# Row maxima of two heads as products, and another order of weight blocks, in an attention and feed-forward kernel

## The chip, the cores and the metric

The kernel runs on one core of a Trainium2 chip. The metric is device microseconds of one execution. Work is done by TensorE (PE, products into PSUM), VectorE (DVE), ScalarE (ACT), GpSimd (POOL) and the DMA engines, whose transfers are here issued by SyncE (SP) alone, one after the other in one queue.

## The reference

Three stages follow one another: attention with a decay, a mixing and feed-forward step, and a second attention by four experts, of which two are chosen for each row. The change touches the first and the part of the second that runs beside it.

```python
# stage 1: q, k, v [4, 8, 576, 64], f [4, 8, 576]
scores = scale * np.matmul(q, k.transpose(0, 1, 3, 2))
cum = np.cumsum(np.log(np.clip(f, 0.0001, 1.0)), axis=-1)
scores = np.where(causal, -1e9, scores + cum[:, :, :, None] - cum[:, :, None, :])
scores = scores - np.max(scores, axis=-1, keepdims=True)
attn = np.exp(scores)
attn = attn / (np.sum(attn, axis=-1, keepdims=True) + 1e-09)
x = np.matmul(attn, v)            # then [4, 576, 512]
# stage 2: U [576, 32], V [32, 576], w_ch1 [512, 2048], w_ch2 [2048, 512]
h = x.transpose(0, 2, 1) @ U @ V
u = x + h.transpose(0, 2, 1)
x = u + np.maximum(u @ w_ch1, 0.0) @ w_ch2
# stage 3: gate, top 2 of 4 experts, causal attention of each, weighted sum
```

## The kernel before

Stage 1 has 32 heads, in 16 pairs; a pair's two heads lie in one set of tiles. Each head has a planned slot of SLOT = 8.4 us. All work of the slots is written as events: `put(h, us, do)` places `do` at `us` in head h's slot, `early(us, do)` places it ahead of the first slot, which begins at FIRST = 15.6. The events are sorted by their planned time (line 1401), and that order is the order in which each engine (PE, DVE, ACT, SP, POOL) executes its instructions. The planned times are only a table that sorts; nothing waits for a clock.

A head goes through these steps:

- **Load and split.** `load_qk` (L865) loads q and k of a pair, 576 KB, into `aside` or `room`. `split_high` (L883 to L887) casts them on ACT into a high part, `split_moves` (L895 to L918) moves rows to other partitions by transfers of 144 KB within the on-chip memory and puts the sums of the decay (4.5 KB, L901) beside them, `split_low` (L932, POOL) makes the low parts. So each head has four tiles: qa, qb, ka, kb.
- **Row maxima.** `last_rows` (L201) and `first_rows_of` (L219) make rough scores, `last_max` (L206) and four `first_max` (L227) take their maxima on DVE into mx, `turn_max` (L233) turns mx on PE into a 5x128 tile mt, `put_row` (L239) copies it on ACT to mr and a transfer of 2.5 KB (L243) puts it as the last row into qa, so that the score products subtract it.
- **Scores.** `score_products` (L285) has a part u = 0 with two pieces of 288 columns and a part u = 1 with four pieces; for each piece there are two products, qa with ka and qb with kb. Exponentials on ACT (L305) and a split into a high cast (L310, ACT) and a low rest (L313, DVE) follow. The odd heads of the first five pairs (NPLAIN) are kept without that split.
- **Values.** Largest absolute value (`value_max`, L363), a turn on PE (`value_turn`, amt, L368), a power of two (`value_power`, L375 to L377), a spread on PE (`value_spread`, rsp, L383), then factors and splits of the values. Weighted sums L341 to L345, or L357.

Between these steps lies work for later stages. `mix_weights` prepares U and V: `low_bits` (L442, L443 on ACT) and `join_bits` (L449, L450 on DVE) put 32-bit words together from two halves, for U (ur, u), for V's two parts (vraw, vst). `weight_events` does the same for eight blocks of the feed-forward weights, t = 0 to 7, from slot 3 on: a read of 512 KB into raw (L457), low bits, join into wst, a cast (L1318, ACT), and a subtraction (L1320, DVE). `busy` (L1358) issues filler products of 128 columns that nobody reads. From slot 10 on the feed-forward runs between the heads (L704, L710, L720); behind head 31, at some 266 us, it runs alone, then stage 3.

## Time and profile before

| | us |
|---|---|
| median of 3 runs | 786.77 (786.45 to 787.19) |
| the profiled execution's own time | 787.25 |
| its span (first to last instruction) | 785.5 |
| first score product of head 0, 1, 2 | 16.77, 23.35, 31.14 |
| first score product of head 6, 14, 31 | 60.62, 126.53, 266.04 |
| first maxima (L206) of head 3, 6, 14 | 30.29, 50.93, 115.69 |

A slot of a head is read from its first product at L285 of 288 columns to that of the next head. The maxima of head n are made two heads ahead, so L206 of head 6 lies in slot 4. A timeline row reads: start, duration, engine, line, operation, output<-input, shapes, count, and in brackets how long the engine was idle before it and what ended that.

### The profile page before, as it was taken

How to read it: one execution, taken by the hardware profiler on the slowest of the kernel's cores; microseconds unless marked ns; L12 is line 12 of the kernel's file. 1: busy time of each engine (PE TensorE's matmuls, PEld its weight loads, DVE VectorE, ACT ScalarE, POOL GpSimd, SP SyncE). 2: the span in 40 equal slices, each digit the busy share in tenths (PEclk: the TensorE clock that was granted, in tenths of full speed). 3: DMA queues.
4: the chain of work that ended last, by engine and by line, in shares of the span. 5: the costliest groups of instructions: out<-in, count | busy, mean ns of one | idle time of the engine just before them, and what ended most of it. 6: DMA issues, size and time to landing. Idle time of an engine off the chain costs nothing.

```text
span 785.5 us, 19296 instructions
## 1 busy us (share of the span) xinstructions
PE 752.3 (96%) x7399; PEld 649.0 (83%) x7399; DVE 598.5 (76%) x1659; ACT 436.1 (56%) x893; POOL 201.9 (26%) x357
## 2 busy tenths in 40 slices
PE   4899999999999999999999999999999999999996
PEld 4799888989998999877777777777778888878873
DVE  6889999999999959988773685366644688887763
ACT  6778887877786725644421242113312366776673
POOL 8734466665564200000020000000000611111110
PEclk9999999999999999999999999999999999999999
DMA  5668665566563165844133224300103475344322
GB/s 163 174 195 227 194 179 169 178 183 180 172 188 116 61 197 184 266 145 168 54 99 109 73 80 158 113 1 1 62 31 76 120 182 139 76 118 97 91 75 95
DMA packets 65708, 101.97 MB, mean 130 GB/s; under 512 B 8864, under 2 KB 43664, under 8 KB 65616
## 3 DMA queue, kind: packets, MB, share of 16 engines
q1 hardware_dynamic: 65248, 100.09, 43.0%
q8 instruction: 58, 0.95, 0.5%
q10 hardware_dynamic: 368, 0.66, 0.3%
q14 instruction: 34, 0.28, 0.1%
HBM read 53.25 MB, written 23.74 MB: 98 GB/s over the span
## 4 chain that ended last, share of the span: by engine, by line
PE 53%; DVE 2%; ACT 1%; issue 0%; DMA 0%; ACTq 0%; DVEq 0%
PE cps L720 17%; PE hps L704 16%; PE pq L1636 6%; PE pv L1680 3%; PE sc L285 3%; PE po L1732 2%; PE ub L219 1%; PE av L341 1%; PE av L345 1%; PE av L343 1%; PE pos L1732 1%; PE ua L201 0%; DVE ph L313 0%; ACT pf L305 0%; DMA out_dram<-ost 0%
## 5 line engine op out<-in xcount | busy, mean ns | idle before, releaser
L709 ACT ACTIVATE hh<-hps 128x288 f16<-128x288 f32 (+1 forms) x128 | 52.4, 410 | 210.6 <-PE hps L704 186.1
L710 DVE SCALAR_TENSOR_TENSOR hl<-hps,hh 128x288 f16<-128x288 f32 (+1 forms) x128 | 58.2, 454 | 79.5 <-ACT hh L709 79.1
L227 DVE CUSTOM_DVE_ANT_0 ub<-ub,maskm 128x448 f32<-128x448 f32 x192 | 82.4, 429 | 2.3 <-PE ub L219 0.7
L285 PE MATMUL sc<-qa,ka 128*128 128x288 f32 (+4 forms) x288 | 72.0, 309 | 1.6 <-DMA qa<-mr 1.1
L726 DVE SCALAR_TENSOR_TENSOR yc<-cps,back,yc 128x288 f32<-128x288 f32 x96 | 49.3, 514 | 24.5 <-PE cps L720 23.0
L285 PE MATMUL sc<-qb,kb 128*128 128x288 f32 (+4 forms) x288 | 63.5, 302 | 0.0
L341 PEld LDWEIGHTS <-ph 128*128 128x128 f16 x645 | 58.9, 97 | 1.2 <-DVE o L422 0.6
L345 PEld LDWEIGHTS <-ph 128*128 128x128 f16 x645 | 59.3, 97 | 0.4 <-DVE ph L313 0.4
L343 PEld LDWEIGHTS <-ph 128*128 128x128 f16 x645 | 59.3, 98 | 0.3
L1863 POOL TENSOR_SCALAR_AFFINE_SELECT pf<-pf 128x128 f32<-128x128 f32 (+1 forms) x80 | 23.9, 318 | 116.3 <-ACT pf L305 115.6
L285 PEld LDWEIGHTS sc<-qb,kb 128*128 128x128 f32 x288 | 52.3, 189 | 1.5
L206 DVE CUSTOM_DVE_ANT_0 ua<-ua,maskm 128x576 f32<-128x576 f32 x48 | 36.5, 761 | 21.0 <-PE ua L201 12.3
L313 DVE TENSOR_TENSOR ph<-pf,ph 128x512 f16<-128x512 f32 (+1 forms) x66 | 47.6, 734 | 6.4 <-ACT ph L310 6.4
L285 PEld LDWEIGHTS sc<-qa,ka 128*128 128x128 f32 x288 | 48.8, 189 | 3.7 <-issue 1.2
L313 DVE TENSOR_TENSOR ph<-aside,ph 128x512 f16<-128x512 f32 (+1 forms) x63 | 49.8, 802 | 1.2 <-ACT ph L310 1.0
L1056 POOL TENSOR_SCALAR_AFFINE_SELECT aside<-aside 128x128 f32<-128x128 f32 (+1 forms) x80 | 39.6, 514 | 38.5 <-ACT aside L305 29.9
L305 ACT ACTIVATE aside<-sc 128x512 f32<-128x512 f32 (+1 forms) x63 | 38.7, 617 | 18.3 <-PE sc L285 16.5
L720 PE MATMUL cps<-hh,w16b 128*128 128x288 f16 x256 | 48.3, 286 | 0.3 <-DVE hl L710 0.3
L720 PE MATMUL cps<-hh,w1lf 128*128 128x288 f16 x256 | 48.4, 286 | 0.0
L720 PE MATMUL cps<-hh,w16a 128*128 128x288 f16 x256 | 48.4, 286 | 0.0
L305 ACT ACTIVATE pf<-sc 128x512 f32<-128x512 f32 (+1 forms) x66 | 39.7, 609 | 13.1 <-PE sc L285 9.4
L720 PEld LDWEIGHTS <-w16b 128*128 128x128 f16 x384 | 37.4, 98 | 10.2 <-issue 0.8
(281 smaller groups left out, 2464.4 us busy)
## 6 DMA issues: line engine op xcount, KB each, us to landing
raw<-in_w_dram SPq DMA_DIRECT2D x32, 512.0 KB
ust<-udram SPq DMA_DIRECT2D x13, 576.0 KB
ydram<-yc SPq DMA_DIRECT2D x10, 576.0 KB
aside<-in_qk_dram SPq DMA_DIRECT2D x8, 576.0 KB
room<-in_qk_dram SPq DMA_DIRECT2D x8, 576.0 KB
udram<-ustage SPq DMA_DIRECT2D x16, 288.0 KB
ydram<-ust SPq DMA_DIRECT2D x8, 576.0 KB
yc<-ydram SPq DMA_DIRECT2D x8, 576.0 KB
```

What stands on the lines that cost most here:

```text
L227: nc.vector.tensor_tensor_reduce(ub[:, bk, off:off + w], ub[:, bk, off:off + w], maskm[:, S - w:S], 1.0, NEG, OP.add, OP.max, mx[:, t:t + 1])
L285: nc.tensor.matmul(ps[:, bk, off:off + w], wa, xa, start=bk not in banks[:n], stop=bk not in banks[n + 1:])
L305: nc.scalar.activation(pf[:, 0:S].rearrange("p (c n) -> p c n", c=2) if whole else pf[:, 0:n], view, AF.Exp, scale=ISC)
L313: nc.vector.tensor_tensor(pl[:, o0:o0 + n], pf[:, 0:n], ph[:, o0:o0 + n], OP.subtract)
L341: nc.tensor.matmul(av[:, it, :], ph[:, c:c + P], vh[:, jt, :], start=first, stop=False)
L343: nc.tensor.matmul(av[:, it, 0:64], ph[:, c:c + P], vl[:, jt, :], start=False, stop=False)
L345: nc.tensor.matmul(av[:, it, :], pl[:, c:c + P], vh[:, jt, :], start=False, stop=last)
L704: nc.tensor.matmul(ph[:], wa[:, k, fs], xa[:, k], start=n == 0, stop=n == 3 * KT - 1)
L709: after(lambda: nc.scalar.activation(hh[:], ph[:], AF.Relu), lambda: nc.vector.scalar_tensor_tensor(hl[:], ph[:], 0.0, high, OP.max, OP.su ...
L710: lambda: nc.vector.scalar_tensor_tensor(hl[:], ph[:], 0.0, high, OP.max, OP.subtract))
L720: nc.tensor.matmul(pc[:], wa[:, t, dsl], xa[:], start=n == 0, stop=n == 3 * FT - 1)
L726: nc.vector.scalar_tensor_tensor(yc[:, d, :], pc[:], back, yc[:, d, :], OP.mult, OP.add)
```

## The change

It has five parts.

1. **Maxima of heads 0 and 1.** No copy and no transfer: `spread_rows` writes, on VectorE, a 5x640 tile with row t of mt at the columns of tile t and zeros elsewhere (mt minus a constant, times the unit matrix), and `score_products` adds for each piece a product of five rows, a tile of -1 with that tile. The four `first_max` of a head stand directly behind one another.
2. **The front.** FIRST is 13.6. Fillers: 76 + 6 + 12 + 8 ahead of slot 0, 8 + 6 in slot 0, 8 + 14 in slots 1 and 2 as before, none in slots 3 to 9. The table of the exponentials is loaded early. Pair 0's amt, power and spread stand ahead of the maxima of head 0. On SP's queue the load of pair 1 stands behind two moves that stood behind it.
3. **Values of other pairs.** The turn (amt) goes from 4.54 to 4.7 and the power from 5.6 to 6.42 of the slot.
4. **U and V.** Bits and joins go to later slots; so do their spread, casts and lows. The split of pair 2's first head goes from slot 0 to slot 1.
5. **Weight blocks.** Every block one slot earlier; for those of an odd slot the read goes to 6.5, the bits to the next slot's 3.2, the join to its 6.45, the cast to the slot behind at 1.4.

The core of the diff:

```diff
-FIRST = 15.6
+FIRST = 13.6
...
+    def spread_rows(mt, w):
+
+        rows = w[0:NT].rearrange("o k n -> o (k n)")[:, 0:SP_]
+        nc.vector.scalar_tensor_tensor(
+            rows.rearrange("o (t p) -> o t p", p=P), mt[:].unsqueeze(1).to_broadcast([NT, NT, P]),
+            PSCALE_LN / ISC, ident[0:NT, 0:NT].unsqueeze(2).to_broadcast([NT, NT, P]),
+            OP.subtract, OP.mult)
+        return rows
+
...
-    def score_products(hb, u, select=False):
+    def score_products(hb, u, select=False, rows=None):
...
+        if rows is not None:
+            todo += [(W[0][1][0:NT, 0, 0:P], rows[:, SP_ - S + i0:SP_ - S + i0 + w], bk, off, w)
+                     for jt, i0, bk, w, off in pieces]
...
         nc.sync.dma_start(f32(qa[lo_, :]), f32(qb[hi_, :]))
         nc.sync.dma_start(f32(ka[lo_, :S]), f32(khigh[hi_, :]))
         if p == 0:
-            rows()
+            split_moves(0, 2)
             load_qk(1)
-            split_moves(0, 2)
         nc.sync.dma_start(f32(kb[lo_, :S]), f32(khigh[hi_, :]))
...
-            st[u] = score_products(hb, u, select)
+            st[u] = score_products(hb, u, select, first_rows.get(h))
...
                 early(us, rows, n)
             early((9.2, 12.45)[h], lambda: last_max(st[0], st["mx"]))
             for n, t in enumerate((3, 2, 1, 0)):
-                early((9.8, 13.1)[h] + 0.6 * n, first, t)
+                early((9.8, 13.1)[h] + 0.02 * n, first, t)
...
         if h == 0:
             early(12.2, turn)
-            early(12.6, lambda: put_row(hb, st["mt"], True))
+            early(12.95, lambda: first_rows.update({h: spread_rows(st["mt"], W[0][2 * h])}))
         else:
             put(h - 1, 0.55, turn)
-            put(h - 1, 1.3, lambda: put_row(hb, st["mt"], True))
+            if h == 1:
+                put(0, 0.58, lambda: first_rows.update({h: spread_rows(st["mt"], W[0][2 * h])}))
+            else:
+                put(h - 1, 1.3, lambda: put_row(hb, st["mt"], True))
...
             early(6.6, step, "am", None, lambda _: value_max(vr))
-            put(0, 0.3, step, "amt", "am", value_turn)
-            put(0, 0.35, step, "full", "amt", value_power)
-            put(0, 2.05, step, "rp", "full", value_spread)
+            early(8.4, step, "amt", "am", value_turn)
+            early(8.45, step, "full", "amt", value_power)
+            early(8.75, step, "rp", "full", value_spread)
...
-        put(h, 4.54, step, "amt", "am", value_turn)
-        put(h, 5.6, step, "full", "amt", value_power)
+        put(h, 4.7, step, "amt", "am", value_turn)
+        put(h, 6.42, step, "full", "amt", value_power)
         put(h + 1, 0.57, step, "rp", "full", value_spread)
         put(h + 1, 2.2, factor)
...
             h = 2 * (p - 2) + j
-            put(h, 4.9, split_high, p, j)
-            put(h, 6.1, split_moves, p, j)
-            put(h, 6.1, split_low, p, j)
+            us = 4.9 if h else SLOT + 2.8
+            put(h, us, split_high, p, j)
+            put(h, us + 1.2, split_moves, p, j)
+            put(h, us + 1.2, split_low, p, j)
...
-        put(2 * (p - 2) - 1 if p > 2 else 0, 0.1, load_qk, p)
+        put(*((2 * (p - 2) - 1, 0.1) if p > 2 else (0, 2.0)), load_qk, p)
...
-        early(1.0, table)
+        early(1.0, table, AF.Ln)
+        early(1.9, lambda: nc.vector.memset(f32(W[0][1][0:NT, 0, 0:P]), -1.0))
+        early(9.5, table, AF.Exp)
...
-        put(0, 4.9, lambda: low_bits(*words(0)))
-        put(0, 5.5, lambda: low_bits(*words(1)))
-        put(0, 8.35, lambda: join_bits(*words(0)))
-        put(1, 0.1, spread)
-        put(1, 2.0, lambda: join_bits(*words(1)))
-        put(1, 2.9, read, 2)
-        put(1, 6.7, high, 0)
-        put(1, 7.9, lambda: low_bits(*words(2)))
-        put(1, 6.8, low, 0)
-        put(2, 2.0, lambda: join_bits(*words(2)))
-        put(2, 6.7, high, 1)
-        put(2, 6.8, low, 1)
+        put(1, 1.4, lambda: low_bits(*words(0)))
+        put(1, 6.5, lambda: low_bits(*words(1)))
+        put(1, 8.35, lambda: join_bits(*words(0)))
+        put(2, 0.1, spread)
+        put(2, 2.0, lambda: join_bits(*words(1)))
+        put(2, 1.9, read, 2)
+        put(2, 6.7, high, 0)
+        put(2, 6.8, low, 0)
+        put(3, 1.4, lambda: low_bits(*words(2)))
+        put(3, 2.75, lambda: join_bits(*words(2)))
+        put(3, 3.4, high, 1)
+        put(3, 3.5, low, 1)
...
-        put(h - 1, 2.9, read)
-        put(h, 8.0 if h % 2 else 6.1, bits)
-        put(h + 1, 2.0, lambda: join_bits(st["to"], pairs_of_words(st["raw"])))
+        late = h % 2
+        put(h - 1, 6.5 if late and t else 2.9, read)
+        put(*((h + 1, 3.2) if late else (h, 6.1)), bits)
+        put(h + 1, 6.45 if late else 2.0,
+            lambda: join_bits(st["to"], pairs_of_words(st["raw"])))
...
-        put(h + 1, 6.7, lambda: nc.scalar.copy(dh, view()))
-        put(*((h + 2, 2.3) if t < 2 * FT - 1 else (h + 1, 8.38)),
-            lambda: nc.vector.tensor_tensor(dl, view(), f32(dh), OP.subtract))
+        put(*((h + 2, 1.4) if late else (h + 1, 6.7)), lambda: nc.scalar.copy(dh, view()))
+        put(h + 2, 2.3, lambda: nc.vector.tensor_tensor(dl, view(), f32(dh), OP.subtract))
...
-    for h in range(10):
-        put(h, 0.54, busy, 8 if h < 3 else 4)
-        if h < 3 or h % 2:
-            put(h, 2.1, busy, 14 if h < 3 else 10)
-    early(12.35, busy, 24)
+    for h in range(3):
+        put(h, 0.54, busy, 8)
+        put(h, 2.1, busy, (6, 14, 14)[h])
+
+    early(3.0, busy, 76)
+    early(8.42, busy, 6)
+    early(10.0, busy, 12)
+    early(12.1, busy, 8)
...
     for t in range(2 * FT):
-        weight_events(0, t, (4, 5, 6, 7, 8, 9, 10, 11)[t])
+        weight_events(0, t, (3, 4, 5, 6, 7, 8, 9, 10)[t])
```

In names of the order, qa_126, qa_130, qa_134 and qa_138 (ka, kb, qb alike) are the tiles of the first four heads (later heads take them again), ph_144 the exponentials of the even heads, mx_90 and mx_96 tiles of maxima, raw the words of a weight block. The line numbers are those of each kernel's own code.

SP's queue at the front, before:

```order
L901 DMA ka_128<-chl 2x1x576
L912 DMA qa_130<-qb_131 64x576
L913 DMA ka_132<-khigh 64x576
L901 DMA ka_132<-chl 2x1x576
L865 DMA room<-in_qk_dram 128x1152
L895 DMA qb_127<-qa_126 64x576
L896 DMA kb_129<-ka_128 64x576
L918 DMA kb_133<-khigh 64x576
L243 DMA qa_126<-mr 1x5x128
```

and now:

```order
L905 DMA ka_128<-chl 2x1x576
L905 DMA ka_132<-chl 2x1x576
L932 DMA qa_130<-qb_131 64x576
L933 DMA ka_132<-khigh 64x576
L913 DMA qb_127<-qa_126 64x576
L914 DMA kb_129<-ka_128 64x576
L877 DMA room<-in_qk_dram 128x1152
L937 DMA kb_133<-khigh 64x576
```

The load into room (pair 1) stood fifth and stands seventh here, behind the moves of qb_127 and kb_129, and the transfer of mr is gone.

ScalarE ahead of and in slot 0, before (from the fill of qa_138 on):

```order
L157 ACTIVATE qa_138<-every 32x640 x2
L239 ACTIVATE mr<-mt 5x128
L883 CAST qa_134<-room 64x576
L884 CAST ka_136<-room 64x576
L886 CAST qb_139<-room 64x576
L887 CAST khigh<-room 64x576
L305 ACT_TABLE_LOAD
L305 ACTIVATE aside<-sc 128x576
L239 ACTIVATE mr<-mt 5x128
L310 CAST ph_144<-aside 128x576
L305 ACTIVATE aside<-sc 128x512
```

and now:

```order
L157 ACTIVATE qa_138<-every 32x640 x2
L1219 ACT_TABLE_LOAD
L1219 ACTIVATE one<-vw_158 1x1
L895 CAST qa_134<-room 64x576
L896 CAST ka_136<-room 64x576
L317 ACTIVATE aside<-sc 128x576
L322 CAST ph_144<-aside 128x576
L898 CAST qb_139<-room 64x576
L899 CAST khigh<-room 64x576
L317 ACTIVATE aside<-sc 128x512
L317 ACTIVATE pf<-sc 128x512
```

The two copies to mr are gone, the table load is ahead, the casts of room's first half still stand ahead of the first exponential, and those of its second half stand between the exponentials of u = 0 and u = 1.

VectorE between head 2's last maximum and head 3's first (L407 in the changed code is L395 before), before:

```order
L395 SCALAR_TENSOR_TENSOR vw_158<-aside,rs,vw_158 128x320
L449 SCALAR_TENSOR_TENSOR u_295<-ur,u_295 128x160
L450 SCALAR_TENSOR_TENSOR u_295<-ur,u_295 128x160
L313 TENSOR_TENSOR ph_144<-aside,ph_144 128x512
L313 TENSOR_TENSOR ph_144<-pf,ph_144 128x512
L449 SCALAR_TENSOR_TENSOR vst<-vraw,vst 96x288
L450 SCALAR_TENSOR_TENSOR vst<-vraw,vst 96x288
L388 RECIPROCAL rs<-rsp 128x1
L206 ISA ua,mx_90<-ua,maskm 128x2x288
```

and now:

```order
L387 TENSOR_REDUCE ar_82<-amt 1x1
L388 TENSOR_SCALAR ar_82<-ar_82 1x1
L389 TENSOR_SCALAR ar_82<-ar_82 1x1
L407 SCALAR_TENSOR_TENSOR vw_158<-aside,rs,vw_158 128x320
L325 TENSOR_TENSOR ph_144<-aside,ph_144 128x512
L325 TENSOR_TENSOR ph_144<-pf,ph_144 128x512
L400 RECIPROCAL rs<-rsp 128x1
L206 ISA ua,mx_90<-ua,maskm 128x2x288
```

The joins of U and of V's first part stand behind head 3's maxima now, and the power of pair 1's values, which stood between two of head 2's maxima, begins this piece.

SP's queue around the load of pair 4 in slot 5, before:

```order
L457 DMA raw<-in_w_dram 128x4x256
L901 DMA ka_128<-cdram 2x576
L907 DMA qb_127<-qa_126 64x576
L908 DMA kb_129<-ka_128 64x576
L865 DMA room<-in_qk_dram 128x1152
L243 DMA qa_134<-mr 1x5x128
L457 DMA raw<-in_w_dram 128x4x256
```

and now:

```order
L881 DMA aside<-in_v_dram 128x320
L905 DMA ka_128<-cdram 2x576
L927 DMA qb_127<-qa_126 64x576
L928 DMA kb_129<-ka_128 64x576
L469 DMA raw<-in_w_dram 128x4x256
L877 DMA room<-in_qk_dram 128x1152
L243 DMA qa_134<-mr 1x5x128
L469 DMA raw<-in_w_dram 128x4x256
```

A weight read stood ahead of the row and the moves and now stands between the moves and the load, in front of the row of head 6's maxima (qa_134<-mr).

## Rows read from the trace of the kernel before

**Rows 1.** The page: busy time, share of the span and instructions of each engine.
```profile
PE 752.3 (96%) x7399; PEld 649.0 (83%) x7399; DVE 598.5 (76%) x1659; ACT 436.1 (56%) x893; POOL 201.9 (26%) x357
```

**Rows 2.** Windows: stretch, length, busy time of each engine, granted clock, DMA share, GB/s.
```profile
39.46:46.85 7.39, 7.35 (x104) 6.96 (x103) 5.26 (x20) 4.23 (x9) 3.51 (x4) 1.00 0.73 211
53.27:60.62 7.35, 7.31 (x104) 6.98 (x103) 6.50 (x22) 5.36 (x11) 3.42 (x4) 1.00 0.69 198
30.29:50.93 20.64, 19.49 (x228) 18.57 (x225) 16.53 (x58) 14.70 (x33) 9.85 (x8) 1.00 0.55 153
50.93:115.69 64.76, 61.28 (x686) 57.98 (x685) 62.11 (x182) 56.19 (x114) 31.51 (x31) 1.00 0.71 206
126.53:261.09 134.56, 130.26 (x1515) 124.05 (x1513) 129.92 (x370) 105.86 (x209) 80.56 (x109) 1.00 0.55 162
261.09:542.00 280.91, 278.91 (x2350) 232.98 (x2349) 195.28 (x458) 100.70 (x197) 10.48 (x28) 1.00 0.36 120
```

**Rows 3.** Timeline of TensorE at the front: start, length, line, output<-input, idle before.
```profile
13.86 2.44 PE L1358 MATMUL some<-every 128*128 128x128 bf16 x24
16.77 0.37 PE L285 MATMUL sc<-qa,ka 128*128 128x288 f32 x1 [0.47 <-DMA qa<-mr]
...
17.56 0.61 PE L1358 MATMUL some<-every 128*128 128x128 bf16 x8
...
21.84 0.76 PE L219 MATMUL ub<-ka,qa 127*128 127x448 f32 x4 [1.12 <-ACT pf L305]
...
23.35 0.37 PE L285 MATMUL sc<-qa,ka 128*128 128x288 f32 x1 [0.65 <-DMA qa<-mr]
```

**Rows 4.** Timeline of SP's DMA issues, front and slot 5.
```profile
10.04 0.39 SPq L865 DMA_DIRECT2D room<-in_qk_dram  x1
...
13.46 0.80 SPq L243 DMA_DIRECT2D qa<-mr  x1
...
53.37 0.54 SPq L865 DMA_DIRECT2D room<-in_qk_dram  x1
54.98 0.75 SPq L243 DMA_DIRECT2D qa<-mr  x1
```

**Rows 5.** Timeline of ScalarE at the front.
```profile
15.48 0.67 ACT L883 CAST qa<-room 64x576 fp32r<-64x576 f32 x1 [2.05 <-DMA room<-in_qk_dram]
...
18.01 1.28 ACT L305 ACT_TABLE_LOAD   x1
19.31 0.65 ACT L305 ACTIVATE aside<-sc 128x576 f32<-128x576 f32 x1
```

**Rows 6.** Timeline of VectorE: the joins of U and V, maxima of heads 4 to 6.
```profile
26.10 1.53 DVE L449 SCALAR_TENSOR_TENSOR u<-ur,u 128x160 int32<-128x160 int32 x1
27.66 0.33 DVE L450 SCALAR_TENSOR_TENSOR u<-ur,u 128x160 int32<-128x160 int32 x1
...
29.23 0.56 DVE L449 SCALAR_TENSOR_TENSOR vst<-vraw,vst 96x288 int32<-96x288 int32 x1
29.83 0.45 DVE L450 SCALAR_TENSOR_TENSOR vst<-vraw,vst 96x288 int32<-96x288 int32 x1
...
37.12 0.77 DVE L206 CUSTOM_DVE_ANT_0 ua<-ua,maskm 128x576 f32<-128x576 f32 x1 [1.08 <-PE ua L201]
...
44.31 0.77 DVE L206 CUSTOM_DVE_ANT_0 ua<-ua,maskm 128x576 f32<-128x576 f32 x1 [1.84 <-ACT g L947]
...
50.93 0.77 DVE L206 CUSTOM_DVE_ANT_0 ua<-ua,maskm 128x576 f32<-128x576 f32 x1 [0.60 <-PE ua L201]
```

**Rows 7.** Waits of VectorE from 50.95 to 115.7: waited for, total, times, longest.
```profile
DVE hl L710 <- ACT hh L709: 0.5, 1, 0.5
DVE ua L206 <- ACT g L947: 0.5, 1, 0.5
```

**Rows 8.** Timeline of VectorE: a block's second join and its subtraction.
```profile
64.15 0.69 DVE L450 SCALAR_TENSOR_TENSOR wst<-raw,wst 128x512 int32<-128x512 int32 x1
64.76 0.69 DVE L1320 TENSOR_TENSOR w1l<-wst,w1h 128x512 fp32r<-128x512 f32 x1
```

More of the change, by code (lines that the diff above doesn't have):

```diff
@@ L887, in split_high, with put_sums @@
             nc.scalar.copy(khigh[hi_, :], tk[hi_])
+    def put_sums(p, j):
+        ka = pair_heads(p)[j][2]
+        src = f32(chl[2 * p + j:2 * p + j + 1]) if p < 2 else cdram[2 * p + j]
+        nc.sync.dma_start(f32(ka[64:66, 0:S]), src)
     def split_moves(p, j):
@@ L898, in split_moves @@
         qa, qb, ka, kb = pair_heads(p)[j]
-        src = f32(chl[2 * p + j:2 * p + j + 1]) if p < 2 else cdram[2 * p + j]
         def rows():
-            nc.sync.dma_start(f32(ka[64:66, 0:S]), src)
+            if p != 1:
+                put_sums(p, j)
+        if p == 0 and j == 0:
+            rows()
+            put_sums(0, 1)
+            return
         if j == 0:
             rows()
-            if p == 0:
-                return
             nc.sync.dma_start(f32(qb[lo_, :]), f32(qa[lo_, :]))
@@ L1024 @@
     events = []
+    first_rows = {}
     def put(h, us, do, *what):
@@ L1173, in split_events @@
                 early(1.2, load_qk, p)
-            early((1.7, 13.4)[p], load_v, p)
-            early((13.45, 13.5)[p], load_second, p)
+            early((1.7, 12.4)[p], load_v, p)
+            put(0, (0.9, 6.5)[p], load_second, p)
+            for j in range(2) if p else ():
+                put(0, (-1.3, 1.9)[j], put_sums, p, j)
             return
-        put(2 * (p - 2) - 1 if p > 2 else 0, 0.1, load_qk, p)
+        put(*((2 * (p - 2) - 1, 0.1) if p > 2 else (0, 2.0)), load_qk, p)
         put(2 * (p - 2), 2.0 if p > 2 else 8.1, load_v, p)
@@ L1188, in fill_zeros, with table @@
                 nc.gpsimd.memset(f32(t_[3 * R:P, :]), 0.0)
-        def table():
-            one_ = small.tile([1, 1], F32, name="one", bufs=1)
-            nc.scalar.activation(one_[:], vws[0][0:1, 1, 0, 64:65], AF.Ln)
+        def table(of):
+            one_ = small.tile([1, 1], F32, name="one", bufs=2)
+            nc.scalar.activation(one_[:], vws[0][0:1, 1, 0, 64:65], of)
         early(0.8, lambda: nc.sync.dma_start(fr, f))
         early(0.9, lambda: nc.vector.memset(ones, 1.0))
-        early(1.0, table)
+        early(1.0, table, AF.Ln)
+        early(1.9, lambda: nc.vector.memset(f32(W[0][1][0:NT, 0, 0:P]), -1.0))
+        early(9.5, table, AF.Exp)
         early(1.5, lambda: nc.vector.memset(maskt[:], 0.0))
```

6 lines of the change are left out of this document (3 added, 3 removed).

## The prediction

> **What bounds the kernel now.** First the engine totals of the page [rows 1]: TensorE is busy for 752.3 of 785.5 us, VectorE for 598.5. That average hides two bounds, and the windows by stage [rows 2] say where each rules. Between the maxima of head 6 (50.93) and of head 14 (115.69) VectorE is busy for 62.11 of 64.76 us and TensorE for 61.28; from 126.53 to 261.09 the two are at 129.92 and 130.26 of 134.56; from 261.09 on TensorE works 278.91 of 280.91 us and VectorE 195.28. A gain made in the first 50 us is carried to the end if these stretches only start earlier and keep their length; nothing behind head 31 is touched. Between 30.29 and 50.93 VectorE works only 16.53 of 20.64 us, so 4.11 us are waiting there, and TensorE is the nearer to full (19.49).
>
> Next the front: TensorE's, the DMA queue's and ScalarE's own timelines [rows 3 to 5]. Head 0's first score product starts at 16.77, held by the row of maxima for 0.47 us; head 1's at 23.35, held by the same transfer for 0.65. On ScalarE head 0's first exponential stands at 19.31 because the casts of pair 1 (the first waits 2.05 us for a load, until 15.48) and then a table load of 1.28 us go ahead.
>
> Last VectorE's starts of the maxima [rows 6]: the four joins of U's and V's words between 26.10 and 30.28 stand ahead of head 3's maxima, and heads 4, 5 and 6 wait 1.08, 1.84 and 0.60 us for their operand.
>
> **Part 1, the rows of maxima.** Two transfers of 2.5 KB leave the path. The first is issued at 13.46 [rows 4]; it is the last wait ahead of 16.77 [rows 3], 3.3 us behind its issue. In their place VectorE writes a 5x640 tile; the nearest row is a join of 96x288 in 0.56 [rows 6], so by elements 640/288 x 0.56 = 1.24 at most and 0.56 at least, I take 0.85. TensorE gets six more products a head, 576 + 1024 columns; eight fillers of 128 columns took 0.61 us, 0.056 each behind the first [rows 3], so 1600/128 x 0.056 = 0.70 us. For head 0 that gives products 3.3 - 0.85 = 2.45 us earlier, at 14.3 instead of 16.77.
>
> **But ScalarE does not follow.** After the change the casts of qa_134 and ka_136, which wait for the load of pair 1, stand ahead of head 0's first exponential, and that load stands behind two moves of 144 KB that were behind it before. 288 KB at 211 GB/s [rows 2] is 1.4 us; at nothing (the queue is backed up anyway) the load lands at 15.48, at the load's own pace (576 KB in 15.48 - 10.04 = 5.44 us [rows 4, 5]) it is 2.7 us more. I take the middle, 16.9. Two casts at about 0.6 then end at 18.1, and the exponential starts at 18.2 to 18.9 against 19.31: the 1.28 us table load has gone to the front, and waiting takes its place. Two more casts and a cast of the exponentials come before u1's exponentials, where one cast stood before. TensorE's products for head 2, held 1.12 us until 21.84 by an exponential [rows 3], stay at about 21.9: of 2.45 us on TensorE almost nothing is left. Head 1's scores lose the wait of 0.65 and begin at some 22.8, 0.55 earlier; its six products lie beside VectorE, which sets slot 1's end.
>
> **Part 2, U and V.** Four joins (1.53 + 0.33 + 0.56 + 0.45 = 2.87 us [rows 6]) leave the stretch ahead of head 3's maxima, whose start goes from 30.29 to about 27.4. They return one head or two later, where VectorE waits now: the 1.08, 1.84 and 0.60 us of [rows 6] are the room. With U's pair behind head 3 the maxima of head 4 come 1.2 earlier (35.9), those of head 5 1.7 (42.6), those of head 6 1.8 (49.1). For TensorE is the nearer bound here (7.35 of 7.39 us from 39.46 [rows 2]), and it gives 0.55 from ahead, the 18 fillers of slots 3 and 4, 18 x 0.056 = 1.0, and at most its idle 20.64 - 19.49 = 1.15, of which I count 0.25: 1.8. The bounds: 0.55, and 2.7 with all of the idle time; 4.1, all of VectorE's waiting, is a rival.
>
> **Part 3, the weight blocks.** Each block still has two bits on ScalarE, two joins and a subtraction on VectorE. They are one head earlier and, for odd heads, half a slot later; between the maxima of heads 6 and 14 only one more subtraction falls, 0.69 us [rows 8]. VectorE does not work for 64.76 - 62.11 = 2.65 us there; the largest two waits are 0.5 each, for the feed-forward's step on ScalarE and for ScalarE's g ahead of a head's maxima [rows 7], the others shorter. Joins at other places may fill them or not: 0 to 2.65, and I take half, 1.3.
>
> **Part 4, the fillers and moves with one answer.** In slots 3 to 9, 68 fillers go: 68 x 0.056 = 3.8 us of TensorE. Those of slots 3 and 4 are in Part 2; the other 50 (2.8 us) hide from 50.93 on beside VectorE, which is the fuller there, so they are worth nothing, and up to 2.8 if VectorE gave way. The power step behind all four maxima and the turn behind the values move a wait of TensorE from one product to the next: zero, and 0.6 either way by the last wait of [rows 6]. They issue no DMA. What moves on SP's queue besides (the second loads of the values, the store of the sums, pair 2's load, V's second read) goes behind the front's transfers and is needed a slot later: zero, and at most the 0.47 us for which such a transfer is late now [rows 3]. Pair 0's power of the values goes ahead of the front's maxima, where VectorE waits: zero; the new table load of 1.28 us [rows 5] lies in ScalarE's wait for pair 1's load: zero, and 1.28 if that load were early.
>
> [...]
> [...]
>
> **Sum.** 1.8 (Parts 1 and 2, to head 6) + 1.3 - 0.69 (Part 3) = 2.4 us. From the profiled run's own 787.25 (span 785.5 and 1.75 around it) that is 784.85; the median before is 786.77, 0.48 below, so 784.3. Own range by the bounds of Parts 2 and 3, one at a time: a gain of 1.8 + 0 - 0.69 = 1.1 to 2.7 + 1.3 - 0.69 = 3.3, so 785.6 to 783.4.
>
> **Rivals.**
> B, the front eats it: the load lands at 18.2, or u1's products, which now share head 0's PSUM buffer and wait for u0's exponential (it stands so in the instruction order), come late; then the 1.8 loses 1 us and Part 3 leaves nothing but its subtraction: gain 1.8 - 1 - 0.69 = 0.1, 786.6. It is also the case in which the change does not do what it says: head 0's products are earlier and nothing follows. For it: 2.05 us of waiting for that load now [rows 5].
> C, more: all of the 4.11 us of VectorE's waiting ahead of 50.93 goes, as the joins fill it and TensorE's products come earlier, 4.1 + 1.3 - 0.69 = 4.7, so 782.0. Against it: TensorE has only 1.15 us idle.
> D, slower: the row of maxima of heads 6, 8 and 10. In slots 5, 7 and 9 a weight read of 512 KB, which waits for joins on VectorE to free its buffer, now stands ahead of the load of 576 KB and the row. Before, the row was issued at 54.98, 1.6 behind the load [rows 4] and 1.7 into its slot of 7.35 us. With two joins (2 x 0.69 [rows 8]) ahead of the read it is issued some 3.0 into the slot. In front the row behind one such load took 3.3 us; behind 512 + 576 KB that is 3.3 x 1088/576 = 6.2, so it lands 9.2 us in, 1.8 behind the next start at 7.4. Three times 1.8, less the 0.3 a slot that VectorE is the later one by, is 4.5 lost: 788.8. It decides where 1088 KB take over 7.4 - 3.0 = 4.4 us, 253 GB/s; the slot from 53.27 moves 198 [rows 2], though for other work too. Against it: the read may find its buffer free, and then it is issued a slot's end earlier, where nothing else is in the queues.
> [...]
> [...]
>
> **How the numbers follow.** Forecast 0.50, B 0.18, C 0.16, D 0.11, E 0.04, 0.01 left. A measurement here tells 0.2%, 1.57 us, from no change: faster means below 785.2, slower above 788.3. Faster: 0.46 of the forecast and all of C, 0.62. Same: the forecast's other 0.04 and B, 0.22. Slower: D, E and the rest, 0.16. The range that leaves out D, E and a little of C: 781.5 to 787.5.
>
> **What would show it.** Right: head 0's first product near 14.3 but its first exponential no earlier than 18; the cast of qa_134 waiting for the load until 16 to 17.5; head 3's maxima at 27 to 28, head 6's near 49, head 14's near 113, all later marks 2.5 earlier. Wrong: a wait for the row of maxima ahead of head 6, 8 or 10 (D), fillers or products at twice their duration behind 40 us (E), head 3's maxima behind 29 (B), or TensorE's idle time before 50 us vanishing together with a gain above 4 (C).

## The result and the profile after

The changed kernel takes 796.43 us (median of 4, 795.3 to 799.76) against 786.72: ratio 1.0128, 95% interval 1.0116 to 1.0141. It is slower, by 9.7 us; the forecast was 784.3. The profiled execution took 795.55, span 793.8.

The page's first line, to be set beside [rows 1]: TensorE is 9.4 us busier, though 68 fillers of the slots are gone.

```profile
PE 761.7 (96%) x7413; PEld 656.8 (83%) x7413; DVE 606.2 (76%) x1662; ACT 437.1 (55%) x892; POOL 202.7 (26%) x357
```

The slots answer where. In the table a slot runs from its first score product to the next head's, in the profiled executions.

| slot | start before | start after | length before | length after |
|---|---|---|---|---|
| 0 | 16.77 | 14.12 | 6.58 | 10.32 |
| 1, 2 | 23.35 | 24.44 | 7.79, 8.32 | 8.36, 7.58 |
| 3, 4 | 39.46 | 40.38 | 7.39, 6.42 | 7.99, 6.37 |
| 5, 6 | 53.27 | 54.74 | 7.35, 7.62 | 10.13, 6.37 |
| 7, 8 | 68.24 | 71.24 | 7.48, 7.63 | 10.30, 6.38 |
| 9, 10 | 83.35 | 87.92 | 7.47, 9.81 | 10.04, 9.52 |
| 11, 12 | 100.63 | 107.48 | 7.97, 8.87 | 9.62, 8.80 |
| 31 | 266.04 | 274.05 | | |

Two places lose: slot 0, which begins 2.65 us earlier and ends 1.1 later, and the odd slots 5, 7, 9 and 11, at 9.6 to 10.3 us where 7.4 to 8.0 stood. Of the even slots 6 and 8 give back 1.25 each, and 4, 10 and 12 at most 0.3. From head 31 on the two kernels differ by 0.3 us.

Slot 0, by windows (columns as in [rows 2]: behind POOL's busy time and count stands the granted clock, then DMA share and GB/s). The clock reads 1.00 up to 18 and 0.50 from there past 24.4 (from 24 to 26 it is 0.79 on average):

```profile
16.00:18.00 2.00, 0.27 (x1) 0.08 (x1) 1.51 (x6) 1.75 (x3) 1.62 (x4) 1.00 1.03 277
18.00:20.00 2.00, 1.91 (x7) 1.82 (x8) 1.66 (x3) 1.94 (x4) 1.86 (x2) 0.51 1.04 235
20.00:22.00 2.00, 2.00 (x12) 1.71 (x11) 0.55 (x1) 0.00 (x1) 1.92 (x2) 0.50 0.89 294
22.00:24.40 2.40, 2.40 (x15) 2.07 (x13) 0.82 (x2) 2.22 (x5) 2.01 (x3) 0.50 1.07 225
```

TensorE's timeline there; 16.85 and 18.09 answer to [rows 3]. Ahead of them it waits 2.12 us for a move, then 0.87 for head 1's maxima and 0.97 for the exponential whose PSUM buffer the second products share. Three products of qa that took 0.72 us in before take 1.22, and six fillers take 0.84 us where eight took 0.61 at a clock of 1.00:

```profile
12.70 0.50 PE L201 MATMUL ua<-ka,qa 127*128 127x288 f32 x2 [2.12 <-DMA ka<-khigh]
...
14.12 0.40 PE L297 MATMUL sc<-qa,ka 128*128 128x288 f32 x1
...
15.37 0.61 PE L1388 MATMUL some<-every 128*128 128x128 bf16 x8
16.85 0.27 PE L233 MATMUL mt<-ident,mx 128*5 128x128 f32 x1 [0.87 <-DVE mx L227]
18.09 1.22 PE L297 MATMUL sc<-qa,ka 128*128 128x320 f32 x3 [0.97 <-ACT aside L317]
...
21.91 0.84 PE L1388 MATMUL some<-every 128*128 128x128 bf16 x6
```

ScalarE's, to be set beside [rows 5]: the casts wait for the load until 16.25 and stand ahead of the first exponential.

```profile
16.25 0.67 ACT L895 CAST qa<-room 64x576 fp32r<-64x576 f32 x1 [4.66 <-DMA room<-in_qk_dram]
...
17.40 0.64 ACT L317 ACTIVATE aside<-sc 128x576 f32<-128x576 f32 x1
...
22.16 0.60 ACT L317 ACTIVATE aside<-sc 128x512 f32<-128x512 f32 x1 [2.15 <-PE sc L297]
```

Slots 4 to 9, the windows that answer to [rows 2]. VectorE is 9.7 of 10.1 us busy in slot 5 and 5.3 to 5.7 of 6.4 in slots 4 and 6; before, it was 6.50 in slot 5 and 7.41 in slot 6. In slots 4 and 6 TensorE is busy all the time (6.37 of 6.37 us), so with this work on it they cannot get shorter. The clock is 0.83 in slot 5 but 1.00 in slot 9, which is as long:

```profile
48.37:54.74 6.37, 6.37 (x57) 6.14 (x56) 5.29 (x17) 6.20 (x14) 1.30 (x1) 1.00 0.71 181
54.74:64.87 10.13, 8.35 (x91) 7.72 (x90) 9.73 (x27) 7.08 (x15) 5.24 (x4) 0.83 0.61 192
64.87:71.24 6.37, 6.37 (x57) 6.11 (x56) 5.69 (x18) 6.20 (x14) 0.75 (x1) 1.00 0.76 198
87.92:97.96 10.04, 7.11 (x91) 6.27 (x88) 9.57 (x27) 7.37 (x15) 6.15 (x4) 1.00 0.62 198
```

VectorE and GpSimd in slot 5. The late block's joins stand ahead of the normalisation (L434), and the second of them takes 1.78 us where the block behind takes 0.69. GpSimd's tensor operation (second list) lies beside it:

```profile
56.19 0.72 DVE L461 SCALAR_TENSOR_TENSOR wst<-raw,wst 128x512 int32<-128x512 int32 x1
56.95 1.78 DVE L462 SCALAR_TENSOR_TENSOR wst<-raw,wst 128x512 int32<-128x512 int32 x1
58.65 0.48 DVE L434 TENSOR_TENSOR room<-av,rn 128x320 f32<-128x320 f32 x1
...
60.25 0.68 DVE L461 SCALAR_TENSOR_TENSOR wst<-raw,wst 128x512 int32<-128x512 int32 x1
60.97 0.69 DVE L462 SCALAR_TENSOR_TENSOR wst<-raw,wst 128x512 int32<-128x512 int32 x1
```

```profile
54.95 1.41 POOL L951 TENSOR_TENSOR qb<-aside,qa 64x576 fp32r<-64x576 f32 x1 [5.28 <-ACT qa L895]
56.44 1.74 POOL L951 TENSOR_TENSOR kb<-aside,ka 64x576 fp32r<-64x576 f32 x1
```

What TensorE waits for from 54.7 to 98: waited for, total, times, longest. The mixing step's sums gp wait for the normalisation three times:

```profile
PE gp L962 <- DVE room L434: 2.8, 2, 1.4
PE gp L962 <- DVE aside L434: 1.5, 1, 1.5
PE up L981 <- DVE g L969: 1.1, 1, 1.1
```

### The profile page after: what moved, and what is told of

It reads as the page before. It is cut to its first block, busy times and chain, and to the rows that moved or that the text cites. A ratio compares the mean times of both kernels' runs of the same rounds, so it can differ in the third digit from the quotient of the medians.

```text
span 793.8 us, 19322 instructions
## 1 busy us (share of the span) xinstructions
PE 761.7 (96%) x7413; PEld 656.8 (83%) x7413; DVE 606.2 (76%) x1662; ACT 437.1 (55%) x892; POOL 202.7 (26%) x357
## 4 chain that ended last, share of the span: by engine, by line
PE 52%; DVE 2%; ACT 1%; issue 0%; DMA 0%; ACTq 0%; DVEq 0%
PE cps L732 17%; PE hps L716 16%; PE pq L1669 6%; PE pv L1713 3%; PE sc L297 3%; PE po L1765 2%; PE ub L219 1%; PE av L353 1%; PE av L357 1%; PE av L355 1%; PE pos L1765 1%; PE ua L201 0%; DVE ph L325 0%; ACT ost L1774 0%; DMA out_dram<-ost 0%
## 5 line engine op out<-in xcount | busy, mean ns | idle before, releaser
L297 PE MATMUL sc<-qa,ka 128*128 128x288 f32 (+4 forms) x288 | 73.6, 316 | 1.0 <-ACT aside L317 1.0
L1896 POOL TENSOR_SCALAR_AFFINE_SELECT pf<-pf 128x128 f32<-128x128 f32 (+1 forms) x80 | 23.8, 318 | 116.4 <-ACT pf L317 115.7
```

The source lines that it names most:

```text
L297: nc.tensor.matmul(ps[:, bk, off:off + w], wa, xa, start=bk not in banks[:n], stop=bk not in banks[n + 1:])
```

## The experiments

Seventeen kernels, with their labels in brackets. Each is set against the kernel before, run in turn with it on the same chip; the ratio is to that kernel's time, with its 95% interval. In the rounds of e16 to e20 single executions of the kernel before took 788.2 to 790.6, five of 45; in the others none was above 787.84.

### The odd slots

**Joins behind the normalisation (e1).** The first theory, W, had the order at one place as the cause.

```diff
-        put(h + 1, 6.45 if late else 2.0,
+        put(h + 1, 6.6 if late else 2.0,
```

> The changed kernel with one number other: the late joins stand at 6.6, just behind the normalisation of the pair's rows at 6.55, no longer just ahead of it at 6.45. Theory W: the normalisation that waits for two joins (2.5 us in slot 5) holds TensorE's sums of the mixing step (waits of 1.37, 1.45, 1.43 us in slots 5, 7, 9) and the idle time halves its clock in slots 5 and 7; with it gone the odd slots fall from 10.1 to some 7.5 and the time from 796.4 to about 789. Rival V: VectorE's work as such is too much in the odd slots (9.7 of 10.1 us busy); the wait moves to the next product that needs VectorE (the turned product with g, or the maxima), odd slots stay above 9 and the time above 794. Rival D: the row of maxima, landing 9.2 us into slot 5, becomes the next wait: odd slots 9.2, about 794, with a wait of the first score product for the transfer of mr.

Measured: 792.94, ratio 1.0078 (1.0061 to 1.0094). The odd slots stay at 9.9 to 10.0, so W falls and V holds for them. The time is below V's 794; of the 3.1 us between the two profiled executions 1.3 lie ahead of slot 1 (23.16 for 24.44), where the two kernels do not differ. The wait at gp is gone, and two others stand in its place:

```profile
PE ub L219 <- ACT ph L1071: 4.7, 3, 1.6
PE up L981 <- DVE g L969: 2.4, 3, 0.8
```

ScalarE shows the first of them: the block's cast (L1349) waits for the joins, and the exponentials that free the buffer of ub stand behind it.

```profile
57.93 0.62 ACT L1349 CAST w1h<-wst 128x512 fp32r<-128x512 f32 x1 [1.77 <-DVE wst L462]
58.46 1.08 ACT L1071 ACTIVATE ph<-sc 128x512 f32<-128x512 f32 x2
```

VectorE is still 9.59 us busy in slot 5, and a join (55.30) takes 1.88. Rival D's transfer is not among the waits.

```profile
53.49:63.48 9.99, 7.14 (x90) 6.25 (x89) 9.59 (x27) 6.98 (x15) 5.78 (x4) 1.00 0.57 181
```

**The old blocks in the changed kernel (e2).** All lines of `weight_events` and the list of slots as before.

> The changed kernel with the weight blocks at the places and slots of before; front, U and V and fillers stay changed. Theories W and V: slots 5 to 13 go back to the lengths of before or a little less; what is left is the front's loss of 1.5 us by slot 4: 787 to 788.5. Rival F (the missing fillers of slots 3 to 9 are what lets the clock fall): the clock still falls in one or two slots, above 790.

Measured: 790.99 (787.81 to 792.43), ratio 1.0046 (1.003 to 1.0063). In the profiled execution slots 5 to 10 have their old lengths (7.09, 7.65, 7.46, 7.64, 7.46, 9.81) and no clock below 1.00 there: F is out for it. For the other executions, which are slower, e12 below tells: with the fillers back the time is the same. But the median is above the range of both theories and the executions lie 4.6 us apart, where the kernel before keeps within 1.1; that leads to the front, below.

**The new blocks alone in the kernel before (e3).**

> The kernel before with the new order of the weight blocks alone; its front and its fillers stay. Theories W and V: the odd slots grow by the wait for the normalisation and, if the clock falls too, by 2.7 each: 791 to 793. Rival F: the fillers at 2.1 of the odd slots fill the wait and hold the clock, so only some 0.7 us a slot is lost: 788 to 789.

Measured: 791.63, ratio 1.0061 (1.0046 to 1.0076), all executions within 0.43 us. As V has it, 791 to 793. The clock is 1.00 throughout, and the odd slots are still 9.92 to 10.03:

```profile
52.97:62.89 9.92, 7.68 (x104) 7.00 (x103) 9.55 (x25) 7.03 (x15) 6.08 (x4) 1.00 0.61 191
62.89:69.28 6.39, 6.39 (x62) 6.28 (x60) 6.22 (x22) 6.22 (x14) 0.38 (x1) 1.00 0.76 207
```

So the weight blocks cost 4.7 us with no help from the clock. Between the starts of slots 5 and 10 VectorE works 41.4 us against 35.9 before. One block more has its joins and subtraction there (2.1 us), and the twelve joins take 13.3 us in all where twelve at 0.69 would take 8.3.

The stretch from slot 5 to the end of slot 13 has the same number of VectorE's instructions in both kernels, all sixteen joins among them (before first, then e3; columns as in [rows 2]):

```profile
53.27:126.53 73.26, 68.73 (x774) 64.92 (x774) 69.33 (x206) 62.17 (x125) 36.21 (x39) 1.00 0.67 194
52.97:130.73 77.76, 68.66 (x774) 64.88 (x774) 73.69 (x206) 62.57 (x126) 39.19 (x39) 1.00 0.61 182
```

It is 4.50 us longer and VectorE is 4.36 us longer busy, so its idle time is nearly the same (3.93 and 4.07). The sixteen joins take 17.25 us for 10.97; other operations of VectorE are nearly 2 us shorter in all. So the loss is joins that take longer, not more work or more waiting: in slots 5, 7 and 9 of e3 the late block's first join takes 1.22 to 1.33 and its second 1.78, each beside a tensor operation of GpSimd.

**Fillers back in the changed kernel (e4).** The loop over ten heads, as before.

> The changed kernel with the 68 fillers of slots 3 to 9 back. Rival F: with 14 fillers ahead of the wait in slots 5, 7 and 9 the clock stays at full speed; the wait itself stays, so 1.8 us in each of slots 5 and 7 come back, and some of slot 9 and 12: about 792. Theory W or V with the clock as a by-product that fillers do not hold: 795 to 797.

Measured: 795.56 (792.81 to 796.45), ratio 1.0105 (1.0084 to 1.0125). Rival F falls: the fillers hold the clock at 1.00 in slot 5, and the slot is hardly shorter (9.94 for 10.13).

```profile
54.45:64.39 9.94, 7.86 (x104) 7.01 (x103) 9.54 (x27) 7.03 (x15) 6.16 (x4) 1.00 0.61 190
```

**All blocks at the places of even heads, one head early (e9).**

```diff
-        late = h % 2
+        late = 0
```

> The changed kernel, with the blocks of odd heads at the same places in a slot as those of even heads (read 2.9, bits 6.1, join 2.0 of the next, cast 6.7, subtraction 2.3), still one head earlier than before. Theory V: two joins and one subtraction a slot instead of four joins in every other one; the odd slots fall from 9.9 or 10 to 7.1 to 7.6, and the time is that of the kernel with the old blocks, 788 to 792. Rival (starting a head earlier costs by itself, or the fillers): odd slots stay above 9, 793 or more.

Measured: 790.16 (787.98 to 796.54), ratio 1.0042 (1.0019 to 1.0064). With one block's joins in each slot the odd slots are 7.59, 8.19 and 8.37, two of them above what was expected, the joins take 0.67 to 0.69 each, and the time is that of the old blocks. Slots 5 to 13 take 73.00 us (before: 73.26). Starting a head earlier is not what costs.

```profile
49.66:56.58 6.92, 6.55 (x58) 6.15 (x56) 6.14 (x18) 6.89 (x15) 2.19 (x2) 1.00 0.51 137
56.58:64.17 7.59, 6.93 (x91) 6.24 (x89) 7.39 (x27) 6.13 (x13) 3.88 (x4) 1.00 0.75 230
64.17:71.17 7.00, 6.60 (x57) 6.15 (x56) 6.23 (x18) 6.97 (x16) 1.71 (x2) 1.00 0.83 210
```

### The front

The six profiled executions that have the changed front and nothing else new ahead of slot 3 (the changed kernel, e1, e2, e4, e9 and e12) start slot 1 at 24.44, 23.16, 22.36, 23.54, 24.16 and 22.37. Theory G put that on the clock, and the clock on the wait of 2.1 to 2.6 us ahead of 12.7. In e1, e2, e4 and e12 the clock does stand at 0.50 between 14 and 16, right behind that wait; in the changed kernel and in e9 it holds until 18 or later and falls behind two shorter ones.

**Pair 1's load ahead of the two moves again (e10).**

> The kernel with the old blocks (e2), and pair 1's load again ahead of the two moves of qb_127 and kb_129, as before the change. Theory G (TensorE waits 2.1 to 2.6 us at 10.6 for the move of ka_132, which lands at 12.6 to 13.1 where it landed at 11.2 before because the two moves behind it share its engines; this idle time halves the clock in slot 0): the wait falls to about 1 us, slot 0 runs at full clock, the load lands about 15.5; 786 to 788 with little spread. Rival (the late landing is not of this order): the wait stays above 2 us, 789 to 792.

Measured: 792.64 (787.85 to 795.89), ratio 1.0064 (1.004 to 1.0087). G's cause for the late move falls: the wait is 2.40 us. A second wait of 2.05 us comes up in slot 0, ahead of the product of qb and kb, whose moves are later now, and the clock is 0.50 from 20 to 24.

For the late move of ka_132 the traces point at another cause, which no run tested: a load of instructions. The changed kernel has one between 9 and 13 us (queue, kind: packets, MB, share of 16 engines); the kernel before has none there:

```profile
q8 instruction: 1, 0.02, 1.6%
```

It is 16 KB on one DMA engine, from 10.33 to 11.33. Of the sixteen parts in which the move lands, fifteen are there by 11.54, and the last comes at 12.56. All twelve kernels with the changed front have such a load, which ends at 11.3 to 11.9, and the last part 1.1 to 1.5 us behind its end. In the seven with the front of before the first such load begins at 21.9 or later, and all parts are there by 11.2. With forty more fillers ahead of it (e11) the next load began at 23.03, for 28.95 in e2. So the fillers ahead of slot 0 seem to have brought a load into the way of the move.

**Head 0's exponential ahead of the casts (e8).** On e2: `(13.0, 14.7, 14.8)` becomes `(14.4, 14.7, 14.8)`.

> The kernel with the old blocks (e2), and head 0's first exponential ahead of the two casts that wait for pair 1's load. If the shared PSUM buffer behind those casts costs (rival B of the prediction): head 0's second products start at 16 to 17 instead of 18.1 to 18.3, slot 1 starts 1 us or more earlier, 788 to 789.5. Theory G: TensorE is at half speed then and busy until 17.7 anyway, so little is gained: within 0.7 us of e2.

Measured: 789.1 (786.49 to 794.33), ratio 1.003 (1.001 to 1.0049). That is in the range of rival B and outside that of G, but the intervals of e8 and e2 overlap, so it does not decide between them. No wait is left within slot 0, but in the profiled execution the clock had fallen by the wait ahead of it (1.88 us), and the slot runs at 0.51 for 9.33 us:

```profile
14.08:23.41 9.33, 9.33 (x48) 8.00 (x47) 5.57 (x15) 5.84 (x11) 7.91 (x10) 0.51 0.97 265
```

**Forty more fillers over the wait for the move (e11).** On e2: `early(10.01, busy, 40)`.

> The kernel with the old blocks (e2), and 40 more fillers (2.2 us at full speed) behind the 12 ahead of head 1's rough scores, so that TensorE is not idle while it waits for the move of ka_132. Theory G: the clock is 1.00 through slot 0, slot 1 starts at 21.5 to 22 in every execution, 786.5 to 788 and all executions within 1 us. Rival (the clock falls from the waits inside slot 0, or not from idle time): the spread of 788 to 792 stays.

Measured: 790.79 (786.81 to 793.6), ratio 1.0047 (1.0028 to 1.0066). The expectation of a narrow spread is missed, as the rival has it. In the profiled execution (786.81, the fastest) of the waits ahead of and in slot 0 only the one of 0.87 for head 1's maxima and one of 0.53 at its end are left, the clock holds, and slot 1 starts at 21.42.

**Fillers of slots 3 to 9 back, without the forty (e12) and with them (e13).** Both on e2.

> The kernel with the old blocks (e2), and the 68 fillers of slots 3 to 9 back. Theory C2 (the executions of e2 to e11 differ by up to 8 us because the clock falls in some of them, in the front or in slots without fillers): fillers in the slots take one of the two sources away; the median falls from 790.8 to 787.5 to 789.5, and a spread of 2 to 3 us from the front stays. Rival (all of the spread comes from the front): 790 to 792 as e2, plus up to 0.8.

> As e12, with the 40 fillers over the front's wait (e11) too. Theory C2: both sources gone, all executions within 1 us of one another, and the front's 1.9 us earlier slot 1 counts: 785 to 787. Rival (the spread has another source than the clock, DMA say): 787 to 793 as e11.

Measured: 790.42 (788.36 to 794.5), ratio 1.0044 (1.0022 to 1.0066), and 791.98 (790.05 to 793.56), ratio 1.0057 (1.0044 to 1.0071). C2 is missed for both. The second profile shows why: the long wait is filled, but the two waits within slot 0 (0.87 and 0.76) remain, the clock falls at about 20 and stays at 0.50 until about 33, through most of slot 1, which takes 11.33 us with TensorE busy all the time.

```profile
14.52:23.48 8.96, 7.33 (x49) 6.01 (x47) 6.37 (x15) 5.96 (x11) 8.02 (x10) 0.79 1.03 256
23.48:34.81 11.33, 11.33 (x101) 10.24 (x100) 5.99 (x20) 5.96 (x13) 2.95 (x5) 0.57 0.51 120
```

**The long wait filled and the shared buffer's wait taken away (e17).** On e12: the forty fillers and the exponential ahead of the casts.

> The change without its weight blocks (old places), with the fillers of slots 3 to 9, with 40 more fillers over the front's wait for the move of ka_132, and with head 0's first exponential ahead of the casts that wait for pair 1's load. Theory G2 (the clock falls in slot 0 behind one of three waits: for the move, for head 1's maxima, for the shared PSUM buffer behind the casts): two of the three are taken away, the clock holds, slot 1 starts at 21 to 21.6 and the executions agree within 1.5 us: 784.5 to 787. Rival (the wait for head 1's maxima, 0.87, or none of the waits, does it): a fall in some executions, 787.5 to 791 with a spread of 3 us or more.

Measured: 788.08, ratio 1.0012 (1.0003 to 1.0021); ten of eleven executions within 0.54 us. G2 holds for the clock: with only the wait for head 1's maxima left of the three (0.88 us), slot 0 takes 6.86 us at 1.00 and slot 1 starts 1.9 us earlier than in before. The time itself is above the expected range. Against e12, which differs only in the forty fillers and the place of the exponential, 2.1 us are gained (3.2 and 1.1 above before).

```profile
14.60:21.46 6.86, 5.46 (x49) 4.54 (x47) 5.25 (x15) 5.34 (x10) 5.83 (x9) 1.00 0.97 244
21.46:29.83 8.37, 7.52 (x102) 6.38 (x101) 5.99 (x20) 5.55 (x12) 4.35 (x5) 1.00 0.83 212
```

### The parts alone

**Fillers of slots 3 to 9 out of the kernel before (e14).**

> The kernel before with the 68 fillers of slots 3 to 9 left out, and nothing else changed. The prediction had them at no cost, with a low chance for the clock falling (rival E). Theory C2: the clock falls in some executions behind the waits of about 1 us in slots 6 and 8; executions from 786 to 792, median 788 to 790. Rival (prediction): 785.5 to 787, with the spread of before, 1.3 us.

Measured: 786.19 (785.5 to 789.74), ratio 0.9994 (0.9982 to 1.0005); eight of ten executions within 1.24 us, two at 789.5 and 789.7. No difference that can be told, and mostly the prediction's case. In the profiled execution slots 3 and 5 are 0.54 and 0.56 shorter and the others as before.

**U and V alone (e15).**

> The kernel before with the later places of U's and V's bits and joins, and nothing else. The prediction's Part 2 has head 3's maxima 2.9 us earlier and head 6's 1.2 to 1.8, 1 us or more at the end: 785 to 785.8. Rival (VectorE's waits behind it take the gain: TensorE sets slots 2 and 3): head 6's maxima within 0.5 us of 50.93 and 786.3 to 787.3.

Measured: 785.75 (785.22 to 786.1), ratio 0.9979 (0.997 to 0.9989). The gain is there: head 3's maxima start at 28.25 (30.29 before), head 6's at 48.82 ([rows 6]: 50.93). Slots 1 and 2 shrink from 7.79 and 8.32 to 7.02 and 7.48, slots 3 to 5 by 0.1 or less. U's first join takes 0.31 where it took 1.53 in [rows 6], when an operation of GpSimd (25.90 to 27.44) lay beside it.

```profile
28.25 0.74 DVE L206 CUSTOM_DVE_ANT_0 ua<-ua,maskm 128x576 f32<-128x576 f32 x1
...
31.27 0.31 DVE L449 SCALAR_TENSOR_TENSOR u<-ur,u 128x160 int32<-128x160 int32 x1
...
48.82 0.77 DVE L206 CUSTOM_DVE_ANT_0 ua<-ua,maskm 128x576 f32<-128x576 f32 x1 [0.60 <-PE ua L201]
```

**U and V, and the fillers of slots 3 to 5 out (e16).**

> The kernel before with the later U and V (e15) and without the fillers of slots 3, 4 and 5 (32 of 128 columns, 1.8 us of TensorE); those of slots 6 to 9 stay. If TensorE is what sets slots 3 to 5, as the windows of before have it, the slots shrink by the fillers and by no more than VectorE allows (1.1 in the kernel without any fillers): 784 to 785.2, with the narrow spread of e15. Rival: VectorE is reached at once, or the clock falls in one execution or another: 785.3 or more, or a spread over 2 us.

Measured: 784.65 (784.29 to 785.23), ratio 0.9969 (0.9958 to 0.998). The lowest of all kernels here, 0.8 us below U and V alone by the ratios, whose intervals overlap; slots 3 and 5 are 0.5 shorter each than in e15. So TensorE was the bound there and held about that much back.

**The rows of maxima alone (e18).**

> The kernel before with the maxima of heads 0 and 1 as products of five rows, and nothing else: its fillers, loads and casts stay where they are. The prediction's Part 1: head 0's products start about 2.4 us earlier and nothing follows from it, since ScalarE's casts and the table load keep the first exponential at 19.3; slot 1 starts at 22.6 to 23.4: 786.3 to 787.3. Rival (the rows are what unsettles the front's clock): slot 0 at half speed in some executions, 788 or more.

Measured: 787.93 (786.92 to 789.89), ratio 1.0005 (0.9993 to 1.0017). No gain; the best execution is as the prediction has it. Head 0's first product starts at 15.93, 0.84 earlier and not 2.4: the fillers of before still stand ahead of it. In the profiled execution the clock falls to 0.50 at about 26, behind two waits of 0.5, and slot 1 takes 10.64 us. Five of the ten executions are above 788, and two of 22 of the kernel before in the same rounds. That the rows unsettle the clock is likely by that, not shown.

**The moved power of the values alone (e19).**

> The kernel before with the turn of the values (amt) at 4.7 and the power at 6.42, and nothing else. The prediction put this move at zero, with 0.6 either way. In the kernel with the front held (e17) the power behind the maxima shows as a wait of 0.21 us of TensorE in each odd slot; if that is a loss, 0.2 in each of up to 15 odd slots: 788 to 790 on this base. If it only takes the place of the wait for the maxima: 786.5 to 787.5.

Measured: 789.6 (788.71 to 791.13), ratio 1.0026 (1.0017 to 1.0035): a loss of 2.4 us. From slot 3 on most odd slots have a new wait that before has nowhere:

```profile
PE mt L233 <- DVE mx L227: 3.8, 5, 1.0
...
PE rsp L383 <- DVE ar L377: 2.0, 10, 0.2
```

while the wait for the maxima (mt) is 3.8 us, and 3.6 in before: the new wait adds to the old one, it does not take its place. Slots 3, 5 and 9 are 0.2 to 0.3 longer than in before and slot 1 is 0.88 longer. The profiled execution is the slowest of the twelve, with the clock at 0.84 in slot 7, so its slots do not add up to the 2.4 us.

**The front held, with the power at its old place and the fillers of slots 3 to 5 out (e20).**

> The front held (e17), with turn and power of the values at their old places and without the fillers of slots 3 to 5. If the 1.9 us that the front gains by slot 1 are lost again to the moved power and those fillers, they come back: slots 3, 5, 7 and 9 shrink to 6.8 to 7.5 and the time is 784 to 785.5, as the kernel with U and V and fewer fillers (e16, 784.65) or better. If the loss is elsewhere (slot 1 at 8.4): 786 to 788.

Measured: 785.3 (785.0 to 788.42), ratio 0.9976 (0.9967 to 0.9986); eleven of twelve within 0.72 us. Slots 5, 7 and 9 are 6.81, 7.46 and 7.47 as expected, slot 3 stays at 7.98. So the change without its weight blocks and its moved power, with the front's waits covered and the fillers of slots 6 to 9 kept, beats the kernel before, and so does e16 with far less.

## Why the prediction was wrong

The differences of the medians from the kernel before, one part at a time: blocks +4.7 (e3), power +2.4 (e19), U and V -1.5 (e15), fillers -1.1 and rows +0.9 (e14 and e18, both within their intervals of none). They make 5.4 of the 9.7. The kernel with the old blocks (e2) is 4.1 above before, and power, U and V, fillers and rows make 0.7 of that. Some 3.4 is left for the rest of the front, by subtraction alone; 2.1 of it come back where the waits of the front are covered and the clock holds (e17 against e12). Parts interact, so these are not exact shares.

- **Part 3, the weight blocks: forecast a gain of 0.6, measured a loss of 4.7.** The step that failed is the price of the joins at their new places: "between the maxima of heads 6 and 14 only one more subtraction falls, 0.69 us", with "0 to 2.65" as the bounds for the rest. That VectorE sets this stretch was right: its idle time from slot 5 through slot 13 is the same in e3 as before. But the same sixteen joins took 17.25 us there for 10.97. The prediction took the price of a join from one row (0.69), though the U join of 1.53 stood in [rows 6] beside another of 0.33, and it drew no bound below nothing. The late joins were planned at 6.45 of the even slots; VectorE came to them 0.9 (e3) to 1.5 us (the changed kernel) into the odd ones, beside GpSimd's operations and in slots that had joins of the even blocks already. How much the crowding of the odd slots cost beside that was not tried: no run has four joins in an odd slot clear of GpSimd. By VectorE's sums little is left for it: its busy time grew by 4.36 us over the nine slots, and their length by 4.50.
- **Part 4, the moved power: forecast zero, "0.6 either way", measured 2.4.** The prediction let the wait move "from one product to the next". In e19 it is a new wait of 0.2 in most odd slots from 3 on, and the old wait for the maxima stays.
- **Part 4, the fillers at no cost:** right (e14), within what can be told. Rival E, a clock that falls in a slot without fillers, was given 0.04; no run shows a slot of 3 to 9 at half the clock throughout. The clock did fall there in places (to 0.50 for 3.4 us each in slots 5 and 7 of the changed kernel, 0.83 over the slot), but e4, with the clock held in slot 5, has that slot only 0.2 shorter. The prediction had no fall of the clock in slot 0, where the change makes new waits. This is the second step that failed: the clock of slot 0 was put at nothing, and by the runs above 2.1 to 3.4 us were lost to it.
- **Part 1 and the front: right in kind, wrong in size.** "But ScalarE does not follow" holds: the first product came at 14.12 (forecast 14.3), the load at 16.25 (16.9), the exponential at 17.40 (18.2 to 18.9). Rival B's shared buffer is there as a wait of 0.97. What fails is "TensorE's products for head 2 ... stay at about 21.9": they came at 23.29, with TensorE's clock at 0.50 from 18.0 on. Head 3's maxima came at 30.79, the sign set for rival B, and had waited 1.78 us for TensorE; head 6's came at 52.23 and head 14's at 122.49 (forecast near 49 and 113). B's price, all but 0.1 us of the gain, was far too low.
- **Part 2, U and V: right in direction, its size partly luck.** Alone it gained 1.5 us at the end and 2.1 at head 6's maxima (forecast 1.8 there). But 1.0 of the forecast 1.8 was for fillers that e15 keeps; its gain comes in slots 1 and 2. With those fillers out (e16) it is 2.4 at the end, inside the bounds of 0.55 to 2.7. Rival C was not seen.
- **Rival D: no such wait.** The row of head 6 was issued 5.04 us into slot 5 (forecast 3.0) and landed 4.2 later (forecast 6.2). So it was there 9.2 into the slot as forecast, by two misses that cancel, and the slot had become 10.1 long. Whether it would bind in a slot of 7.5 with this queue order was not tried.

The join at 56.95 takes 1.78 us and ends at 58.73, 0.55 behind the end of GpSimd's operation of 64x576 (58.18); the joins at 60.25 and 60.97, with no operation of GpSimd beside them, take 0.68 and 0.69. In the kernel before, where none of the sixteen joins lies beside such an operation, each takes 0.68 or 0.69. The U join of 1.53 in [rows 6] lies beside one (25.90 to 27.44), so a look at what GpSimd does where the joins go would have raised their price. That GpSimd's operation is the reason was not tried by moving it.

## What to carry to other kernels

Price an operation at its new place by what runs beside it there, not by its duration at the old one. Here the order of the weight blocks cost 4.7 us though VectorE executed the same instructions: joins of 0.69 us took up to 1.9 beside GpSimd's operations, on the engine that set the pace. A planned place is not the place in time: VectorE ran behind its plan, and joins planned for even slots ran in odd ones. Look also at who stands behind the moved operation in the other queues. New waits on TensorE can cost more than their own length: in the changed kernel the clock was at 0.50 for 6.8 us behind two waits of 0.87 and 0.97, and slot 0 took 10.32 us for 6.58. Covering one of several such waits was not enough (e11, e13), covering two of three was (e17).
